# Reading TensorE's weights with a step in a gated attention and feed-forward kernel

## The chip, the cores and the metric

The kernel runs on one core of one Trainium2 chip. A core has TensorE (matrix products, into PSUM), VectorE, ScalarE and GpSimd (elementwise work), SyncE (which issues the transfers here), an on-chip memory SBUF of 128 partitions, and PSUM. In the profile they are PE, PEld (TensorE's loads of weights, which overlap its products), DVE, ACT, POOL and SP. A product takes two operands from SBUF: the weights, which are loaded into the array first (128 columns at most), and the moving operand, which then streams past them. The metric is the time of one execution on the device in microseconds; lower is better.

## The reference

Two blocks read the same x of 2048 tokens by 448, and a gate per token mixes them. Everything is float32.

```python
g = _sigmoid((x * gate_w).sum(-1, keepdims=True))
a = _A_ref(x, A_wqkv, A_wo)             # 16 heads of 28: softmax(q k^T * 28**-0.5) v, then @ wo
b = _B_ref(x, B_w_gate, B_w_up, B_w_down)   # (gelu(x @ w_gate) * (x @ w_up)) @ w_down, 1792 features
return g * a + (1 - g) * b
```

## The kernel before

**Precision.** Products that need float32 are made from two parts of each operand in a faster 32-bit type (float32r): a rounded part and the remainder. A product is then the sum of three: rounded by rounded, remainder by rounded, rounded by remainder. As the inner size 448 is three blocks of 128 and a half block of 64, the list `PAIRS` names eleven matmuls for one output tile: three pairs of blocks each for three combinations, and two in which the half block's two parts share 128 rows. So `X` has seven blocks of 2048 tokens (three rounded, one mixed, three remainders), and a weight tile has eight blocks of 128 columns. A tile that holds weights for a product and is followed by `LINE` (8) floats of padding is shifted against its neighbours by 32 bytes.

**Every matmul goes through the helper `mm` at L48**, which keeps them in the order of the program. So all products show L48 in the profile and are told apart by their tiles.

**Stage 1, queries, keys and values** (to about 117 us). `load_wqk` (L91 to L95) loads one of seven tiles of the q and k weights and splits it into `WQK`: ScalarE writes the rounded part (L94), VectorE the remainder (L95). `load_x` splits x into `X` (L107 to L114). `qk_tile` makes q and k with `WQK` as weights and `X` moving (group pqk, 7 tiles by 4 token blocks of 512, 11 matmuls each); the results go to memory. `v_tile` (L129 to L134) makes the values of 128 tokens with `X` as weights and `WV` moving (group pv, 16 tiles of 11 matmuls); column 448 of its result is the gate's argument.

**Stage 2, attention** (about 117 to 776 us). For each of 16 heads and 16 tiles of 128 keys, `scores` multiplies keys `K` (weights) with queries `Q` (moving), two matmuls for each half of the queries (group sc), and ScalarE takes the exponential (L265). `values` multiplies `V` (weights of 32 columns, four column groups side by side) with the exponentials; these operands are plain float32, and each such product is two instructions in the profile (group po). They are issued in batches for four key tiles at once. Between the scores, a generator `up` issues the up-projection of the feed-forward block, matmul by matmul, and three feature blocks of the gate projection: `half` tiles (one block of 128 features, split by `load_half`, L230 to L237, both halves by VectorE at L235 and L236) are the weights and `X` is moving (group pu, 68 tiles of 11 matmuls). The order of all this is written out in the loops; each `half` tile is loaded one feature block before it is used.

**Stage 3, gate, down and output** (about 776 us to the end). `hidden` makes the gate projection of the other 11 feature blocks (group pg, `half` tiles as weights, the rounded part written by ScalarE through `by_act` at L240), takes the gelu, multiplies by the up-projection and splits the product into `hl` (rounded and remainder, 512 tokens each). `down` multiplies `hl` (weights, 128 tokens at a time) with the down weights `w` (moving, 448 columns; group pd, 672 matmuls) and adds to `acc`, and after the last feature blocks writes out 128 tokens per transfer (L418). `load_o` and `project` do the attention's output projection with the split attention output `O` as weights and `WO` moving (group pd from ohl, 176 matmuls).

The matmuls' distance is what one counts in a chain that runs through TensorE: the start of one to the start of the next. The weights of a product are loaded while the product before it streams.

Of the kernel before, what the change touches and what calls it, by code (L numbers as in the profile page):

```python
# [7 lines left out]
F32 = mybir.dt.float32  # L8
# [3 lines left out]
OP = mybir.AluOpType  # L12
# [5 lines left out]
P = 128  # L18
TB = 512
# [8 lines left out]
RATE = 2  # L28
NB = 3
ORDER = (2, 3, 1, 4, 0, 5, 6)  # L30
NR = 4 * DH + 2
LINE = 8
VW = 450
# [4 lines left out]


PAIRS = [(b, w) for b in range(3) for w in (b, 4 + b)] + [(4 + b, b) for b in range(3)] + [(3, 3), (3, 7)]  # L40


@with_exitstack
def gated_mix(ctx: ExitStack, tc: tile.TileContext, xT, wqk, wvg, wg, wu, wd, wo, sel, ident, out):
    nc = tc.nc

    def mm(o, lhsT, rhs, start, stop):
        tc.keep_in_program_order(nc.tensor.matmul(o, lhsT, rhs, start=start, stop=stop))  # L48
# [10 lines left out]
    X = keep.tile([P, 7, S + LINE], F32R, name="X")  # L59
# [5 lines left out]
    kq = attn.enter_context(tc.tile_pool(name="kq", bufs=1))  # L65
    heads = [tuple(kq.tile([NR, S + (i + 1) * LINE], F32R, name=f"{x}{i}")[:, 0:S] for x in "QK")
             for i in range(2)]
# [5 lines left out]
    with ExitStack() as ph:  # L73
# [4 lines left out]
        psb = ph.enter_context(tc.tile_pool(name="psb", bufs=1, space=PSUM))  # L78

        WQKS = wp.tile([P, NQK, 8 * P + 2 * LINE], F32R, name="WQK")  # L80
        WQK = WQKS[:, :, 0:8 * P].rearrange("p t (w n) -> p t w n", w=8)
        WV = wp.tile([P, 8, VW], F32R, name="WV")
        selt = wp.tile([P, NQK, H], F32, name="selt")
        mx = wp.tile([P, NQK, NTB], F32, name="mx")
# [6 lines left out]
        def load_wqk(t):  # L91
            r = raw(wqk[t])
            r = r.rearrange("p (b n) -> p b n", b=4)
            nc.scalar.activation(WQK[:, t, 0:4], r, AF.Copy)  # L94
            nc.vector.tensor_tensor(WQK[:, t, 4:8], r, WQK[:, t, 0:4].bitcast(F32), OP.subtract)  # L95

# [19 lines left out]
        def qk_tile(t, tb):  # L116
            s = slice(tb * TB, (tb + 1) * TB)
            p = ps.tile([P, TB], F32, name="pqk")
            for i, (x, w) in enumerate(PAIRS):
                mm(p, WQK[:, t, w, :], X[:, x, s], i == 0, i == len(PAIRS) - 1)  # L120
            hl = st.tile([P, 2, TB], F32R, name="hl", bufs=3)
# [7 lines left out]
        def v_tile(i):  # L129
            p = psv.tile([P, VW], F32, name="pv")  # L130
            for j, (x, w) in enumerate(PAIRS):
                mm(p, X[:, x, i * P:(i + 1) * P], WV[:, w, :], j == 0, j == len(PAIRS) - 1)
            nc.scalar.activation(V[:, i, :, 0:DH], p[:, 0:D].rearrange("p (h d) -> p h d", h=H), AF.Copy)
            nc.vector.tensor_copy(gate[:, 0, i:i + 1], p[:, D:D + 1])  # L134

# [17 lines left out]
        for i in range(4):  # L153
            v_tile(i)
# [6 lines left out]
        for i in range(4, NT):  # L161
            v_tile(i)
# [6 lines left out]
        for a in range(2):  # L169
            nc.vector.tensor_copy(sh[:, a, :], hcol[:, a:a + 1].bitcast(F32).to_broadcast([H, P]))  # L170
            nc.sync.dma_start(out=shd[:, a].rearrange("h (i n) -> h i n", n=P),
                              in_=sh[:, a:a + 1].to_broadcast([H, NT, P]))
# [24 lines left out]
    with tc.If(bounded < 1):  # L197
        with ExitStack() as ph:
# [5 lines left out]
            for h in range(H):  # L204
                Q = gp.tile([4 * DH, S], F32R, name="gQ")
                K = gp.tile([4 * DH, S], F32R, name="gK")
# [3 lines left out]
                for i in range(NT):  # L210
                    p = gps.tile([P, S], F32, name="gsc")
                    for c in range(S // 512):
# [11 lines left out]
                                  in_=ms.bitcast(F32))  # L224
# [3 lines left out]
    halves = {}  # L228

    def load_half(src, f, key, hi):  # L230
        raw = fw.tile([P, 4, P], F32, name="hraw")
        w = fw.tile([P, 8 * P + LINE], F32R, name="half", bufs=3)
        w = w[:, 0:8 * P].rearrange("p (w n) -> p w n", w=8)
        nc.sync.dma_start(out=raw, in_=src[f])
        hi(w[:, 0:4], raw)  # L235
        nc.vector.tensor_tensor(w[:, 4:8], raw, w[:, 0:4].bitcast(F32), OP.subtract)  # L236
        halves[key, f] = w  # L237

    def by_act(o, i):
# [3 lines left out]
    with ExitStack() as ph:  # L243
# [14 lines left out]
        def scores(h, kt, half):  # L258
            Q, K = heads[h % 2]
            sc = psc.tile([P, 1024], F32, name="sc")  # L260
            for c in range(2):
                mm(sc[:, c * 512:(c + 1) * 512], K[:, kt * P:(kt + 1) * P],
                   Q[:, half * 1024 + c * 512:half * 1024 + (c + 1) * 512], True, True)
            pt = pp.tile([P, 1024], F32, name="pt")
            nc.scalar.activation(pt, sc, AF.Exp, scale=SCALE)  # L265
            PT[h, kt, half] = pt
# [29 lines left out]
        def up():  # L296

            todo = [(wu, f, "u") for f in range(NF)] + [(wg, f, "g") for f in range(NB)]
            load_half(*todo[0], nc.vector.tensor_copy)
            for n, (_, f, key) in enumerate(todo):  # L300
                for tb in range(NTB):
                    if tb == 1 and n + 1 < len(todo):
                        load_half(*todo[n + 1], nc.vector.tensor_copy)
                    s = slice(tb * TB, (tb + 1) * TB)
                    p = psu.tile([P, TB], F32, name="pu")
                    for i, (x, w) in enumerate(PAIRS):
                        mm(p, halves[key, f][:, w], X[:, x, s], i == 0, i == len(PAIRS) - 1)
                        if i < len(PAIRS) - 1:
                            yield False
                    u = op.tile([P, TB], F32, name="u")  # L310
                    nc.vector.tensor_copy(u, p)  # L311
                    nc.sync.dma_start(out=ud[n, :, s], in_=u)
                    yield True

        filler = up()

        hold = 0
# [9 lines left out]
        def spaced(h, kt, half):  # L327
            nonlocal hold
            scores(h, kt, half)
            hold = max(hold - 1, 0)  # L330
# [4 lines left out]
        for h in range(H):  # L335
            for kt in range(NKT):
                if kt == 2 and h + 1 < H:
                    load_head(h + 1)
                for half in range(2):
# [6 lines left out]
                    elif count != LATE - 1 or h + kt == 0:  # L346
                        first, last = h == 0 and kt <= ENDS[0] + 1, h == H - 1 and kt > ENDS[-2]
# [13 lines left out]
    with ExitStack() as ph:  # L361
# [9 lines left out]
        def load_f(f):  # L371
            if f >= NB:
                load_half(wg, f, "g", by_act)
            draw = gp.tile([P, D], F32, name="draw")
            w = gp.tile([P, 2 * D + LINE], F32R, name="w", bufs=3)
            w = w[:, 0:2 * D].rearrange("p (a n) -> p a n", a=2)
            nc.sync.dma_start(out=draw, in_=wd[f * P:(f + 1) * P])
            nc.scalar.activation(w[:, 0], draw, AF.Copy)
            nc.vector.tensor_tensor(w[:, 1], draw, w[:, 0].bitcast(F32), OP.subtract)
            WD[f] = w  # L380

        def hidden(f, tb, hl):
            s = slice(tb * TB, (tb + 1) * TB)
            u = tp.tile([P, TB], F32, name="u")
            nc.sync.dma_start(out=u, in_=ud[f, :, s])
            g = tp.tile([P, TB], F32, name="g")
            if f < NB:
                pg = tp.tile([P, TB], F32, name="gs")
                nc.sync.dma_start(out=pg, in_=ud[NF + f, :, s])
            else:  # L390
                pg = psg.tile([P, TB], F32, name="pg")
                for i, (x, w) in enumerate(PAIRS):
                    mm(pg, halves["g", f][:, w], X[:, x, s], i == 0, i == len(PAIRS) - 1)
            nc.scalar.activation(g, pg, AF.Gelu_apprx_tanh)  # L394
            nc.vector.tensor_tensor(g, g, u, OP.mult)  # L395
            nc.scalar.activation(hl[:, 0], g, AF.Copy)  # L396
            nc.vector.tensor_tensor(hl[:, 1], g, hl[:, 0].bitcast(F32), OP.subtract)  # L397

        def down(c, tb, hls):
            for i in range(4):  # L400
                t = tb * 4 + i
                s = slice(i * P, (i + 1) * P)
                p = psd.tile([P, D], F32, name="pd")
                n = 3 * len(hls)
                k = 0
                for f, hl in hls:
                    for a, b in ((0, 0), (1, 0), (0, 1)):
                        mm(p, hl[:, a, s], WD[f][:, b], k == 0, k == n - 1)
                        k += 1
                g1 = gate[:, 2, t:t + 1]  # L410
                if c == 0:
                    nc.vector.tensor_scalar(acc[:, t], p, g1, None, OP.mult)
                elif c < NF // FC - 1:
                    nc.vector.scalar_tensor_tensor(acc[:, t], p, g1, acc[:, t], OP.mult, OP.add)  # L414
                else:
                    y = tp.tile([P, D], F32, name="y")
                    nc.vector.scalar_tensor_tensor(y, p, g1, acc[:, t], OP.mult, OP.add)  # L417
                    nc.sync.dma_start(out=out[0, t * P:(t + 1) * P], in_=y)  # L418


        WO = wpo.tile([P, 8, D], F32R, name="WO")
# [23 lines left out]
        def project(tb):  # L445
            O = OHL[tb]
            for i in range(4):
                t = tb * 4 + i
                p = psd.tile([P, D], F32, name="pd")
                for k, (x, w) in enumerate(PAIRS):  # L450
                    mm(p, O[:, x, i * P:(i + 1) * P], WO[:, w], k == 0, k == len(PAIRS) - 1)
                nc.vector.scalar_tensor_tensor(acc[:, t], p, gate[:, 1, t:t + 1], acc[:, t], OP.mult, OP.add)

        order = [f for c in ORDER for f in range(c * FC, (c + 1) * FC)]
        load_f(order[0])
# [56 lines left out]
```

## Time and profile before

| | us |
|---|---|
| median of 3 runs | 1065.9 (1065.82 to 1066.63) |
| the profiled execution | 1066.95 |
| its span, first to last instruction | 1065.2 |
| TensorE busy in it | 1053.1 |
| ScalarE busy | 616.6 |
| VectorE busy | 320.8 |
| GpSimd busy | 41.1 |
| mean granted TensorE clock | 0.997 |

The profile is one execution, recorded by the hardware. A group of instructions is given as line, engine, operation, output<-inputs, shape and count, then busy microseconds, the mean nanoseconds of one, and the idle time of the engine before them with what ended it. Matmuls are pipelined and the ends of their records are modelled, so the mean duration of a matmul is longer than its share of the time. The chain that ended last is followed back from the last instruction, and a view of it in order of time merges neighbours of one group: start, microseconds, and how many. A view of stages gives, for each stretch of the span, its length, then the busy time of PE, PEld, DVE, ACT and POOL with counts, the granted clock, and the transfers' share.

### The profile page before, as it was taken

To read this page: it belongs to the slowest core of one execution; us is meant where nothing else is said; L and a number is where in the kernel's file an instruction comes from. 1 tells how busy PE (TensorE), PEld (TensorE's weight loads), DVE (VectorE), ACT (ScalarE), POOL (GpSimd) and SP (SyncE) were. 2 spreads that over 40 slices of the span, in tenths; PEclk is the share of its full clock that TensorE was granted. 3 is DMA by queue.
4 is the path that set the end of the run, shared out by engine and by line. 5 is a ranking of instruction groups with operands and counts; after the bars stand their busy time and mean duration, and the time that the engine had idled before them with its cause. 6 is when DMAs were issued, how large, how long until landed. Compare 5 with 4: busy or idle time off the path is not lost.

```text
span 1065.2 us, 14545 instructions
## 1 busy us (share of the span) xinstructions
PE 1053.1 (99%) x5664; PEld 733.4 (69%) x5664; DVE 320.8 (30%) x519; ACT 616.6 (58%) x732; POOL 41.1 (4%) x32
## 2 busy tenths in 40 slices
PE   7999999999999999999999999999999999999998
PEld 6889756556556556556566565565588888889887
DVE  6651111111111110110110110110157656577555
ACT  6422478778777777777787787787633332233321
POOL 5300000000000000000000000000001011100000
PEclk9999999999999999999999999999999999999999
DMA  8975222332332332332332232331164323342223
GB/s 278 302 262 121 59 73 73 120 103 73 100 106 73 96 110 73 94 112 73 94 112 74 94 111 74 94 102 42 59 192 138 106 88 94 92 148 67 62 85 118
DMA packets 58907, 115.85 MB, mean 109 GB/s; under 512 B 12784, under 2 KB 18160, under 8 KB 55216
## 3 DMA queue, kind: packets, MB, share of 16 engines
q1 hardware_dynamic: 58832, 114.85, 34.8%
q8 instruction: 47, 0.77, 0.3%
q14 instruction: 28, 0.23, 0.1%
HBM read 74.44 MB, written 40.37 MB: 108 GB/s over the span
## 4 chain that ended last, share of the span: by engine, by line
PE 88%; DVE 0%; issue 0%; DVEq 0%
PE sc L48 24%; PE po L48 21%; PE pu L48 16%; PE pd L48 16%; PE pg L48 11%; DVE u L311 0%; DVE y L417 0%; DVE gate L181 0%; DVE gate L180 0%; DVE gate L182 0%; DVEq L311 0%
## 5 line engine op out<-in xcount | busy, mean ns | idle before, releaser
L265 ACT ACTIVATE pt<-sc 128x1024 f32<-128x1024 f32 x512 | 482.3, 1026 | 165.3 <-PE sc L48 164.7
L48 PE MATMUL sc<-Q,K 114*128 114x512 f32 x1024 | 317.9, 402 | 1.3 <-issue 1.3
L48 PEld LDWEIGHTS sc<-Q,K 114*128 114x128 f32 x1024 | 188.8, 189 | 94.6 <-issue 54.5
L48 PE MATMUL pu<-X,half 128*128 128x512 f32 x748 | 238.3, 397 | 0.4 <-DVE u L311 0.3
L48 PE MATMUL po<-pt,V 128*32 128x512 f32 x2048 | 233.0, 595 | 0.0
L311 DVE COPY u<-pu 128x512 f32<-128x512 f32 x68 | 47.1, 692 | 493.2 <-PE pu L48 486.3
L48 PEld LDWEIGHTS pu<-X,half 128*128 128x128 f32 x748 | 141.4, 190 | 35.4 <-issue 1.4
L48 PEld LDWEIGHTS po<-pt,V 128*32 128x32 f32 x2048 | 60.0, 109 | 138.2 <-issue 132.4
L48 PE MATMUL pd<-w,hl 128*128 128x448 f32 x672 | 140.4, 365 | 0.0
L48 PEld LDWEIGHTS pd<-w,hl 128*128 128x128 f32 x672 | 126.1, 188 | 11.7
L48 PE MATMUL pg<-X,half 128*128 128x512 f32 x484 | 115.9, 394 | 0.0
L48 PEld LDWEIGHTS pg<-X,half 128*128 128x128 f32 x484 | 90.9, 188 | 20.1
L48 PE MATMUL pqk<-X,WQK 128*128 128x512 f32 x308 | 74.4, 404 | 6.0 <-ACT X L107 6.0
L48 PEld LDWEIGHTS pqk<-X,WQK 128*128 128x128 f32 x308 | 59.2, 193 | 20.7 <-ACT X L107 6.9
L394 ACT ACTIVATE g<-pg 128x512 f32<-128x512 f32 x44 | 26.2, 595 | 74.8 <-PE pg L48 74.7
L395 DVE TENSOR_TENSOR g<-g,u 128x512 f32<-128x512 f32 x56 | 46.4, 836 | 54.0 <-ACT g L394 53.5
L396 ACT ACTIVATE hl<-g 128x512 fp32r<-128x512 f32 x56 | 35.2, 630 | 42.9 <-DVE g L395 37.1
L414 DVE SCALAR_TENSOR_TENSOR acc<-pd,gate,acc 128x448 f32<-128x448 f32 x80 | 52.9, 679 | 6.3 <-PE pd L48 6.3
L442 POOL TENSOR_TENSOR ohl<-oraw,ohl 128x1536 fp32r<-128x1536 f32 x4 | 14.0, 3512 | 755.3 <-ACT ohl L438 755.3
L397 DVE TENSOR_TENSOR hl<-g,hl 128x512 fp32r<-128x512 f32 x56 | 38.3, 688 | 10.6 <-ACT hl L396 8.7
L48 PE MATMUL pv<-WV,X 128*128 128x450 f32 x176 | 36.8, 369 | 0.0
L48 PE MATMUL pd<-WO,ohl 128*128 128x448 f32 x176 | 36.6, 366 | 0.0
(60 smaller groups left out, 325.2 us busy)
## 6 DMA issues: line engine op xcount, KB each, us to landing
ud<-u SPq DMA_DIRECT2D x68, 256.0 KB
qkd<-hl SPq DMA_DIRECT2D x28, 512.0 KB
Q<-qkd SPq DMA_DIRECT2D x64, 224.0 KB
K<-qkd SPq DMA_DIRECT2D x64, 224.0 KB
u<-ud SPq DMA_DIRECT2D x56, 256.0 KB
raw<-in_xT SPq DMA_DIRECT2D x16, 256.0 KB
rb<-rdend SPq DMA_DIRECT2D x64, 64.0 KB
hraw<-in_wu SPq DMA_DIRECT2D x14, 256.0 KB
```

Source lines behind the costliest of these rows:

```text
L48: tc.keep_in_program_order(nc.tensor.matmul(o, lhsT, rhs, start=start, stop=stop))
L265: nc.scalar.activation(pt, sc, AF.Exp, scale=SCALE)
L311: nc.vector.tensor_copy(u, p)
L394: nc.scalar.activation(g, pg, AF.Gelu_apprx_tanh)
L395: nc.vector.tensor_tensor(g, g, u, OP.mult)
L396: nc.scalar.activation(hl[:, 0], g, AF.Copy)
L397: nc.vector.tensor_tensor(hl[:, 1], g, hl[:, 0].bitcast(F32), OP.subtract)
L414: nc.vector.scalar_tensor_tensor(acc[:, t], p, g1, acc[:, t], OP.mult, OP.add)
L442: nc.gpsimd.tensor_tensor(O[:, 4:7], o[:, 0:3], O[:, 0:3].bitcast(F32), OP.subtract)
```

## The change

Every float32r operand that serves as weights of a product is read with a step between its columns. Moving operands stay as they were.

- `WQK`: the eight blocks of a tile are interleaved column by column, so that the 128 columns of a block lie 8 floats (32 bytes) apart. ScalarE and VectorE write them in this way.
- `half` tiles: within each of four blocks the rounded part and the remainder alternate, so columns lie 2 floats (8 bytes) apart; the two writers write with that step.
- `X` in `v_tile`, `K` in `scores`, `hl` in `down` and `O` in `project`: the layout stays, and the 128 tokens of a tile are no longer neighbours but every fourth of a block of 512 (`tokens`), 4 floats (16 bytes) apart. The rows of `V`, the gate and `acc` follow this order, and the transfers of the output write every fourth row.

`V` in `values` is weights too and stays as it was. The padding stays.

```diff
+def tokens(i):
+    first = i // 4 * TB + i % 4
+    return slice(first, first + 4 * (P - 1) + 1, 4)
...
-        WQK = WQKS[:, :, 0:8 * P].rearrange("p t (w n) -> p t w n", w=8)
+        WQK = WQKS[:, :, 0:8 * P].rearrange("p t (n w) -> p t w n", w=8)
...
-                mm(p, X[:, x, i * P:(i + 1) * P], WV[:, w, :], j == 0, j == len(PAIRS) - 1)
+                mm(p, X[:, x, tokens(i)], WV[:, w, :], j == 0, j == len(PAIRS) - 1)
...
-        w = w[:, 0:8 * P].rearrange("p (w n) -> p w n", w=8)
+        w = w[:, 0:8 * P].rearrange("p (b n a) -> p a b n", b=4, a=2)
         nc.sync.dma_start(out=raw, in_=src[f])
-        hi(w[:, 0:4], raw)
-        nc.vector.tensor_tensor(w[:, 4:8], raw, w[:, 0:4].bitcast(F32), OP.subtract)
+        hi(w[:, 0], raw)
+        nc.vector.tensor_tensor(w[:, 1], raw, w[:, 0].bitcast(F32), OP.subtract)
...
-                mm(sc[:, c * 512:(c + 1) * 512], K[:, kt * P:(kt + 1) * P],
+                mm(sc[:, c * 512:(c + 1) * 512], K[:, tokens(kt)],
                    Q[:, half * 1024 + c * 512:half * 1024 + (c + 1) * 512], True, True)
...
-                        mm(p, halves[key, f][:, w], X[:, x, s], i == 0, i == len(PAIRS) - 1)
+                        mm(p, halves[key, f][:, w // 4, w % 4], X[:, x, s], i == 0, i == len(PAIRS) - 1)
...
-                    mm(pg, halves["g", f][:, w], X[:, x, s], i == 0, i == len(PAIRS) - 1)
+                    mm(pg, halves["g", f][:, w // 4, w % 4], X[:, x, s], i == 0, i == len(PAIRS) - 1)
...
-                s = slice(i * P, (i + 1) * P)
+                s = tokens(i)
...
-                    nc.sync.dma_start(out=out[0, t * P:(t + 1) * P], in_=y)
+                    nc.sync.dma_start(out=out[0, tokens(t)], in_=y)
...
-                    mm(p, O[:, x, i * P:(i + 1) * P], WO[:, w], k == 0, k == len(PAIRS) - 1)
+                    mm(p, O[:, x, tokens(i)], WO[:, w], k == 0, k == len(PAIRS) - 1)
```

## The prediction

> **What bounds the kernel now.** I read the page from the top: busy times, the slices with the granted clock, the chain that ended last, then the groups.
>
> ```profile
> span 1065.2 us, 14545 instructions
> PE 1053.1 (99%) x5664; PEld 733.4 (69%) x5664; DVE 320.8 (30%) x519; ACT 616.6 (58%) x732; POOL 41.1 (4%) x32
> ...
> PEclk9999999999999999999999999999999999999999
> ...
> PE 88%; DVE 0%; issue 0%; DVEq 0%
> PE sc L48 24%; PE po L48 21%; PE pu L48 16%; PE pd L48 16%; PE pg L48 11%; DVE u L311 0%; DVE y L417 0%; DVE gate L181 0%; DVE gate L180 0%; DVE gate L182 0%; DVEq L311 0%
> ```
>
> TensorE is busy 99% of the span at the full granted clock, and the chain runs from matmul to matmul with nearly nothing else in it. So the kernel gets shorter only if the distance from one matmul to the next shrinks, and longer as soon as it grows. The number of matmuls stays as it is. The next view is the groups: the matmuls, and the weight loads (PEld) that run beside them.
>
> ```profile
> L48 PE MATMUL sc<-Q,K 114*128 114x512 f32 x1024 | 317.9, 402 | 1.3 <-issue 1.3
> L48 PE MATMUL pu<-X,half 128*128 128x512 f32 x748 | 238.3, 397 | 0.4 <-DVE u L311 0.3
> L48 PE MATMUL po<-pt,V 128*32 128x512 f32 x2048 | 233.0, 595 | 0.0
> L48 PEld LDWEIGHTS po<-pt,V 128*32 128x32 f32 x2048 | 60.0, 109 | 138.2 <-issue 132.4
> L48 PE MATMUL pd<-w,hl 128*128 128x448 f32 x672 | 140.4, 365 | 0.0
> L48 PEld LDWEIGHTS pd<-w,hl 128*128 128x128 f32 x672 | 126.1, 188 | 11.7
> L48 PE MATMUL pg<-X,half 128*128 128x512 f32 x484 | 115.9, 394 | 0.0
> L48 PEld LDWEIGHTS pg<-X,half 128*128 128x128 f32 x484 | 90.9, 188 | 20.1
> L48 PE MATMUL pqk<-X,WQK 128*128 128x512 f32 x308 | 74.4, 404 | 6.0 <-ACT X L107 6.0
> L48 PE MATMUL pv<-WV,X 128*128 128x450 f32 x176 | 36.8, 369 | 0.0
> L48 PE MATMUL pd<-WO,ohl 128*128 128x448 f32 x176 | 36.6, 366 | 0.0
> ```
>
> The edit reaches every group here but po, whose weights V stay as they are: pu and pg (748 + 484 = 1232, the half tiles, step 8 bytes); sc, pv and both pd (1024 + 176 + 672 + 176 = 2048, step 16); pqk (308, step 32). That is 3588 matmuls: 2564 with 512 moving columns (sc, pu, pg, pqk), and 1024 with 448 or 450 (pd, pv). A mean duration (394) is no distance, as matmuls overlap. The distances stand in the chain by time, in a stretch where gate matmuls and down matmuls alternate:
>
> ```profile
> 841.05 5.09 PE pg L48 x22
> 846.14 4.88 PE pd L48 x24
> ```
>
> 5.09/22 = 231.4 ns for 512 columns, 4.88/24 = 203.3 ns for 448. The difference, 28.0 ns over 64 columns, is 0.438 ns a column. 512 columns at that are 224.3, so 7.1 ns of each matmul do not go with its columns. This line through two points is one measure of what each matmul pays beside its stream. A second comes from po, in the timeline of TensorE, where sixteen of its instructions are four rounds of four side by side:
>
> ```profile
> 235.88 1.90 PE L48 MATMUL po<-pt,V 128*32 128x512 f32 x16
> ```
>
> The last round lasts about the mean of 0.595, so a round takes (1.90 - 0.595)/3 = 0.435 us for 512 columns. These operands are plain float32, and one such instruction lasts 595 - 397 = 198 ns longer than pu's with as many columns. I read that as two steps per column against one, which makes a bare stream of 512 columns 435/2 = 217.5 ns: an estimate, and 231.4 - 217.5 = 13.9 ns less than pg's distance. So 7 to 14 ns in each of the 3588 matmuls are not explained by columns. In po a weight load brings 32 columns; in the other groups a load of 128 columns goes beside every stream.
>
> [...]
>
> **The change, part by part.** *Weight loads.* No instruction is added or removed; 3588 loads read their 128 columns 2, 4 or 8 elements apart while the moving operand is read as before. No row shows an operand read or written with a step, so this is the unknown cost, and I bound it from both sides. On the good side, the unexplained time of each matmul may be the load and the stream in each other's way in the memory; a load that hops through it no longer walks behind the stream in the same place. What it can give back is between 7.1 and 13.9 ns a matmul: 25.5 to 49.9 us. I take the middle, 10.5 ns: 3588 x 10.5 = 37.7 us. The middle, because the two measures have equal weight: the line through two points counts what depends on columns as lost for good, the other calls everything above po's rate removable. On the bad side a column may take longer to read, or both collide more often; those are the rivals, and their ends stand there.
>
> *Writes with a step.* load_wqk writes 7 + 7 times with step 32, load_half 28 times with step 8.
>
> ```profile
> L94 ACT ACTIVATE WQK<-raw 128x512 fp32r<-128x512 f32 x7 | 4.3, 629 | 2.4 <-DMA raw<-in_wqk 2.3
> L95 DVE TENSOR_TENSOR WQK<-raw,WQK 128x512 fp32r<-128x512 f32 x7 | 4.6, 687 | 4.7 <-ACT WQK L94 4.6
> L235 DVE CAST half<-hraw 128x512 fp32r<-128x512 f32 x17 | 7.1, 418 | 0.0
> L236 DVE TENSOR_TENSOR half<-hraw,half 128x512 fp32r<-128x512 f32 x28 | 19.3, 691 | 7.4 <-ACT half L240 6.9
> L240 ACT ACTIVATE half<-hraw 128x512 fp32r<-128x512 f32 x11 | 6.9, 629 | 7.5 <-PE pu L48 7.4
> ```
> ```profile
> 0.00:20.00 20.00, 14.00 (x49) 10.73 (x50) 12.10 (x17) 13.60 (x22) 10.62 (x12) 1.00 0.76 248
> ...
> 117.00:776.00 659.00, 657.27 (x3825) 390.73 (x3824) 87.41 (x150) 485.39 (x519) 0.00 (x0) 1.00 0.29 89
> 776.00:1056.00 280.00, 280.00 (x1310) 245.72 (x1309) 176.56 (x263) 89.15 (x142) 16.88 (x8) 1.00 0.36 107
> ```
> ```profile
> 3.50 0.63 ACT L94 ACTIVATE WQK<-raw 128x512 fp32r<-128x512 f32 x1 [1.47 <-DMA raw<-in_wqk]
> 4.78 0.63 ACT L107 ACTIVATE X<-raw 128x512 fp32r<-128x512 f32 x1 [0.66 <-DMA raw<-in_xT]
> 5.47 1.22 PE L48 MATMUL pqk<-X,WQK 128*128 128x512 f32 x2 [5.47 <-ACT X L107]
> ```
>
> The second fence is the stages: span, then busy PE, PEld, DVE, ACT, POOL. Each write may stay as it is or, as the far end, take twice its time. The half tiles then cost DVE up to 7.1 + 19.3 = 26 us more and ACT 7, spread over 935 us in which DVE is busy for 264 and ACT for 574; each tile is loaded a whole feature block ahead. That work is hidden by the matmuls of the block before, so I cost it at nothing; without that cover its price would be those 33 us. The WQK tiles are needed at the start, where PE is idle for 6 of 20 us: ACT idled 0.66 us between the first WQK tile and X, so that tile's doubling just fits, and the first matmul waits for X. The other six could push ACT back by 6 x 0.63 = 3.8 us, while PE works through the first tiles. Between 0 and 3.8 us I take 0.6, one such copy, as PE has 11 matmuls per tile to cover the rest.
>
> *Steps taken from a whole block* (X, K, hl, O): tokens(i) picks every fourth token of the same 512, so each matmul waits for the tiles it waited for before; no DMA, wait or queue entry is added, and none is moved past another. *Output*: the same 16 transfers, their rows now 4 tokens apart in memory.
>
> ```profile
> out<-y SPq DMA_DIRECT2D x16, 224.0 KB
> ```
>
> Rows of 448 floats stay whole; only the last one is bare, and with rows as long as before I take 0 (between 0 and 1 us). *What comes next when matmuls move closer*: ScalarE's exponentials, 512 of 1026 ns.
>
> ```profile
> L265 ACT ACTIVATE pt<-sc 128x1024 f32<-128x1024 f32 x512 | 482.3, 1026 | 165.3 <-PE sc L48 164.7
> ```
> ```profile
> 235.50 3.57 PE po L48 x32
> ...
> 245.59 3.57 PE po L48 x32
> ```
>
> A round of the attention lasts 245.59 - 235.50 = 10.09 us and holds 8 exponentials, 8.2 us. Besides po's 3.57 us it holds 28 matmuls; 14 ns off each make 9.7 us, still above 8.2. ScalarE does not become the bound.
>
> *Sum*: the profiled execution took 1066.95 us (span 1065.2 and 1.75 around it), 1.05 above the median of the runs, 1065.9. 1066.95 - 37.7 + 0.6 = 1029.9, and against the median 1028.8: I say 1029.
>
> **The rivals.** *The read becomes the bound (slower).* Loads of 128 columns take 188 ns, po's of 32 take 109: (188 - 109)/96 = 0.82 ns a column, 105 for 128. In the groups a load of pd leaves 11.7 us/672 = 17 ns idle, one of pg 20.1/484 = 42. If a load must end before its matmul starts, the distance grows once a column costs 17/128 = 0.14 ns more. Were a column read to take twice as long, a load would be 293 and the distance 293 + 17 = 310: 1332 matmuls of 512 (sc, pqk) lose 78.6, 1024 of pd and pv 106.7, together 214 us, so 1280. For it: pd's small idle time. Against it: loads overlap one another where they may.
>
> ```profile
> L48 PEld LDWEIGHTS pr<-selt,sq 128*1 128x1 f32 x14 | 0.4, 81 | 0.0
> ```
>
> 14 loads of 81 ns lie in 0.4 us, so the fixed 81 is latency, and only the 105 must fit: doubled, 210 against 203.3, 7 ns for 1024 matmuls, 1073. I price both. [...]
>
> *More collisions (slower).* The 7.1 ns may be the price of the memory that a load touches, which grows to 2, 4 and 8 times: 7.1 x (1232 x 1 + 2048 x 3 + 308 x 7) = 67.7 us, 1134; at 13.9 ns 1198. For it: the loads are the only thing each of these matmuls has beside its stream. Against it: nothing shows that the price goes with the stretch.
>
> *Nothing happens.* If loads and streams never meet, the distance stays and only the start changes: 1066.5. [...] The unexplained 7 to 14 ns speak against, without naming the load.
>
> **How the numbers follow.** Faster, with 1029 and a range of its own from 1005 (17 ns a matmul: 14, and 3 for rounding and for the starts of a round's four that lie apart) to 1055: 0.60. Unchanged: 0.08. The read as bound, strictly (1280): 0.11; overlapped (1073): 0.08. More collisions (1134 and above): 0.13. A difference under 0.2%, 2.1 us, can't be told from none. So faster 0.60, same 0.08, slower 0.32. From 1005 to 1135 the range leaves out the strict bound (0.11), half of the collisions (0.06) and 0.03 below.
>
> **What would show it.** Right: pg's 22 matmuls in the chain near 4.86 us and pd's 24 near 4.63, po's 32 still 3.57, loads still 188. Wrong: loads well over 188 in sc and pd but not in pu (the read binds); loads of 188 with pg's 22 above 5.09 (collisions); ACT or DVE waiting for WQK in the first 20 us (writes); or an idle PE in the attention with ScalarE full. The weakest step is the first: that the unexplained time belongs to the load at all.

## The result and the profile after

The changed kernel takes 1115.45 us (median of 4 runs, 1114.6 to 1116.13) against 1066.27 for the kernel before (median of 4): the ratio is 1.0458, 95% interval 1.044 to 1.0476, or 48.8 us more (4.58% of 1066.27; the costs of the other kernels below are worked out from their ratios in the same way). The forecast was 1029, so it had the wrong sign. TensorE is busy for 99% of the span as it was, and the clock is the same:

```profile
span 1114.1 us, 14545 instructions
PE 1101.6 (99%) x5664; PEld 867.5 (78%) x5664; DVE 327.6 (29%) x519; ACT 622.9 (56%) x732; POOL 42.2 (4%) x32
...
PEclk9999999999999999999999999999999999999999
...
PE sc L54 23%; PE po L54 21%; PE pd L54 18%; PE pu L54 16%; PE pg L54 10%; DVE u L317 0%; DVE y L423 0%; DVE gate L187 0%; DVE gate L186 0%; DVE gate L188 0%; DVEq L317 0%
...
L54 PE MATMUL sc<-Q,K 114*128 114x512 f32 x1024 | 329.1, 413 | 1.3 <-issue 1.3
L54 PEld LDWEIGHTS sc<-Q,K 114*128 114x128 f32 x1024 | 275.0, 311 | 69.5 <-issue 54.5
L54 PE MATMUL pu<-X,half 128*128 128x512 f32 x748 | 239.9, 400 | 0.3
L54 PE MATMUL pd<-w,hl 128*128 128x448 f32 x672 | 161.3, 397 | 0.0
L54 PEld LDWEIGHTS pd<-w,hl 128*128 128x128 f32 x672 | 160.0, 330 | 0.8
L54 PEld LDWEIGHTS pg<-X,half 128*128 128x128 f32 x484 | 94.9, 196 | 16.8
L54 PE MATMUL pqk<-X,WQK 128*128 128x512 f32 x308 | 78.5, 418 | 6.6 <-ACT X L113 5.7
L54 PEld LDWEIGHTS pqk<-X,WQK 128*128 128x128 f32 x308 | 76.5, 329 | 8.2 <-ACT X L113 7.1
L54 PE MATMUL pv<-WV,X 128*128 128x450 f32 x176 | 42.0, 400 | 0.0
```

(Lines have moved by six: L54 is the helper `mm`.) Weight loads are what changed. With steps of 16 and 32 bytes they last 311 to 332 ns instead of 188 to 193; with 8 bytes 196 to 197. The chain in order of time, in the stretch that the prediction used, gives the distances:

```profile
835.60 5.13 PE pg L54 x22
840.73 5.62 PE pd L54 x24
846.35 5.12 PE pg L54 x22
```

The gate matmuls, with half tiles as weights, are where they were: 5.12/22 = 233 ns against 231. The down matmuls went from 203.3 to 5.62/24 = 234.2. One more place grows, the first pair of score matmuls behind a batch of po. In the timeline of the kernel before, no load had run for 0.84 us ahead of such a pair's first one, so there is nothing that it overlaps. Here is the pair before, behind the batch that begins at 235.50, and one after:

```profile
239.07 0.67 PE sc L48 x2
239.73 0.47 PE pu L48 x2
```
```profile
237.27 3.57 PE po L54 x32
240.84 0.80 PE sc L54 x2
241.64 0.47 PE pu L54 x2
```

The sum by groups, for pd the difference of the distances, for the others that of the mean durations: pd 848 x 30.9 ns = 26.2 us, pv 176 x 31 = 5.5, sc 1024 x 11 = 11.3 (8.3 of it the 64 first pairs, 0.13 each), pqk 308 x 14 = 4.3, pu and pg 2.7. Together 50.0, against 48.9 by the spans.

### The profile page after: what moved, and what is told of

It is laid out like the page before. It is cut to its first block, busy times and chain, and to the rows that moved or that the text cites. A ratio compares the mean times of both kernels' runs of the same rounds, so it can differ in the third digit from the quotient of the medians.

```text
span 1114.1 us, 14545 instructions
## 1 busy us (share of the span) xinstructions
PE 1101.6 (99%) x5664; PEld 867.5 (78%) x5664; DVE 327.6 (29%) x519; ACT 622.9 (56%) x732; POOL 42.2 (4%) x32
## 4 chain that ended last, share of the span: by engine, by line
PE 88%; DVE 0%; issue 0%; DVEq 0%
PE sc L54 23%; PE po L54 21%; PE pd L54 18%; PE pu L54 16%; PE pg L54 10%; DVE u L317 0%; DVE y L423 0%; DVE gate L187 0%; DVE gate L186 0%; DVE gate L188 0%; DVEq L317 0%
## 5 line engine op out<-in xcount | busy, mean ns | idle before, releaser
L54 PE MATMUL sc<-Q,K 114*128 114x512 f32 x1024 | 329.1, 413 | 1.3 <-issue 1.3
L54 PEld LDWEIGHTS sc<-Q,K 114*128 114x128 f32 x1024 | 275.0, 311 | 69.5 <-issue 54.5
L54 PE MATMUL pu<-X,half 128*128 128x512 f32 x748 | 239.9, 400 | 0.3
L54 PE MATMUL po<-pt,V 128*32 128x512 f32 x2048 | 233.0, 595 | 0.0
L54 PEld LDWEIGHTS po<-pt,V 128*32 128x32 f32 x2048 | 60.0, 109 | 130.7 <-issue 127.0
L54 PE MATMUL pd<-w,hl 128*128 128x448 f32 x672 | 161.3, 397 | 0.0
L54 PEld LDWEIGHTS pd<-w,hl 128*128 128x128 f32 x672 | 160.0, 330 | 0.8
L54 PEld LDWEIGHTS pu<-X,half 128*128 128x128 f32 x748 | 147.0, 197 | 15.8 <-issue 1.4
L54 PE MATMUL pg<-X,half 128*128 128x512 f32 x484 | 116.4, 395 | 0.0
L54 PEld LDWEIGHTS pg<-X,half 128*128 128x128 f32 x484 | 94.9, 196 | 16.8
L54 PE MATMUL pqk<-X,WQK 128*128 128x512 f32 x308 | 78.5, 418 | 6.6 <-ACT X L113 5.7
L54 PEld LDWEIGHTS pqk<-X,WQK 128*128 128x128 f32 x308 | 76.5, 329 | 8.2 <-ACT X L113 7.1
L400 ACT ACTIVATE g<-pg 128x512 f32<-128x512 f32 x44 | 26.2, 596 | 86.7 <-PE pg L54 86.6
L54 PE MATMUL pd<-WO,ohl 128*128 128x448 f32 x176 | 42.1, 398 | 0.0
L54 PE MATMUL pv<-WV,X 128*128 128x450 f32 x176 | 42.0, 400 | 0.0
L54 PEld LDWEIGHTS pd<-WO,ohl 128*128 128x128 f32 x176 | 41.9, 332 | 0.0
```

## The experiments

Two theories stood at the start. *Slow read*: a column that lies 16 bytes or more from the last one takes about twice as long to read; reads overlap the stream before, and a matmul waits only where its stream is shorter than the read. *Collisions*: a load with a step disturbs the stream beside it. A third question was what the 7 to 14 ns were that the prediction had set out to win.

**A table of patterns (scan).** Extra matmuls into a PSUM bank that nothing reads, 24 for each pattern, for 64 and then 512 moving columns:

```diff
+        for N in (64, 512):
+            for k in range(24):
+                keep_(nc.tensor.matmul(px[0:P, 0:N], step(k % 7, 1), X[:, (k + 3) % 7, 0:N], start=True, stop=True))
...
+            for k in range(24):
+                keep_(nc.tensor.matmul(px[0:P, 0:N], step(k % 7, 16), X[:, (k + 3) % 7, 0:N], start=True, stop=True))
```

> The kernel before with 768 extra matmuls behind the values of stage 1, into a PSUM bank that nothing reads: for 64 and then for 512 moving columns, sixteen patterns of 24 each. Weights from X with steps of 1, 1 (one float further on), 2, 2 (one float further on), 3, 4, 5, 6, 8 and 16 floats, then 32 and 64 columns side by side, then step 1 with a moving operand that is one column repeated, step 1 with a moving operand read with step 2, and bfloat16 weights with steps of 2 and of 16 bytes. Slow read (the read of a column takes about twice as long once its neighbour lies 16 bytes away or more, and reads overlap the stream before): at 64 moving columns the distance is the read alone, about 109 ns for steps 1 and 2, 230 to 245 for 4 and above, 3 in between; at 512 columns 232 for steps 1 and 2 and 235 to 245 from 4 on. Collisions (a stepped load delays the stream and is not slower itself): at 64 columns all steps about 109, at 512 columns a distance that grows from step to step. On the unexplained 7 to 14 ns: if they belong to the load, 32 columns in place of 128 bring 512 moving columns from 232 to about 218; if they are the two operands meeting in the memory, the repeated column does so too; if they belong to neither, both stay at 232.

In the part with 64 columns the granted clock falls to half behind the first pattern, as the view of stages shows in its third column from the end. L174 is the first pattern, step 1 (in floats), still at the full clock; L184 is step 4, at half of it.

```profile
120.00:123.00 3.00, 3.00 (x27) 2.94 (x25) 0.76 (x4) 0.76 (x2) 0.00 (x0) 1.00 0.00 0
138.00:143.00 5.00, 5.00 (x25) 5.00 (x25) 0.00 (x0) 0.00 (x0) 0.00 (x0) 0.50 0.00 0
```
```profile
120.58 2.76 PE L174 MATMUL px<-X 128*128 128x64 f32 x24
143.44 5.79 PE L184 MATMUL px<-X 128*128 128x64 f32 x24
```

24 matmuls are 23 distances and one duration, so a distance is (busy - mean)/23, good to about 2 ns. The load sets it here, as weights of 32 columns in place of 128 bring it to some 54 ns (L194). It is 108 ns for step 1 at the full clock (mean duration 273 ns). At half the clock it is 213 ns for step 1 (L198, whose weights are side by side) and for steps 2 and 3, but 234 for 4 (mean 420), 223 for 5 and 6, 239 for 8 and 218 for 16. At the full clock step 4 takes 235 as well (L213 of the second table below). So a load of columns side by side took twice as long at half the clock (213 ns against 108), and a load of columns 16 bytes apart did not get longer (234 against 235). Collisions had expected the same distance for all steps.

The part with 512 runs at the full clock (1.00 from 190 to 240 us). Groups by line, loads first: busy, then the mean of one. L176 is step 1 from one float further on (the first pattern, L174, ran into the change of the clock), L178 step 2, L182 step 3, L184 step 4, L186 step 5, L190 step 8, L192 step 16 (in floats).

```profile
L190 PEld LDWEIGHTS px<-X 128*128 128x128 f32 x24 | 6.0, 330 | 0.0
L186 PEld LDWEIGHTS px<-X 128*128 128x128 f32 x24 | 5.8, 305 | 0.0
L192 PEld LDWEIGHTS px<-X 128*128 128x128 f32 x24 | 5.7, 301 | 0.0
L184 PEld LDWEIGHTS px<-X 128*128 128x128 f32 x24 | 5.7, 310 | 0.0
L182 PEld LDWEIGHTS px<-X 128*128 128x128 f32 x24 | 5.6, 253 | 0.0
L178 PEld LDWEIGHTS px<-X 128*128 128x128 f32 x24 | 4.6, 194 | 0.9
L176 PEld LDWEIGHTS px<-X 128*128 128x128 f32 x24 | 4.5, 188 | 1.1
```

Less the fixed 81 ns that the prediction read from pr, 128 columns take 107 ns at step 1, 113 at 2, 172 at 3, 229 at 4, 220 to 249 above. In pieces of 16 bytes these are 32, 64, 96 and 128 pieces: 113/64, 172/96 and 229/128 are all 1.8 ns a piece. So these float32r loads took the larger of 0.83 ns a column (107/128) and about 1.8 ns a piece; beyond one column per piece the step changed it by no more than a tenth (218 to 239 ns at 64 columns), and what makes this difference is open. In L213, where the load holds the matmuls up, its record is longer (331 ns, 250 less 81, at a distance of 235), so there the distance is the better measure. The bfloat16 patterns of the table do not fit this: their 128 columns loaded in 98 ns when side by side and in 144 when 16 bytes apart, although the latter touch 128 pieces too (L202 and L204, at 512 columns). With 512 columns the distance is 231 to 239 ns at every step but that of 32 bytes, 247; it does not grow from step to step as collisions asked.

The same table's matmuls answer the third question (L198: the moving operand is one column repeated; L194: weights of 32 columns; L200: a moving operand of step 2):

```profile
L200 PE MATMUL px<-X 128*128 128x512 f32 x24 | 11.1, 634 | 0.0
L176 PE MATMUL px<-X 128*128 128x512 f32 x24 | 5.8, 396 | 0.0
L194 PE MATMUL px<-X 128*32 128x512 f32 x24 | 5.7, 394 | 0.0
L198 PE MATMUL px<-X 128*128 128x512 f32 x24 | 5.3, 379 | 0.0
```

By (busy - mean)/23 the distances are L176 235 ns, L194 231, L198 214, L200 455. A quarter of the weights changes next to nothing; a moving operand that reads one place gives back the whole excess (214), and so does one of bfloat16, half the bytes (L204, 5.3 us and 379 ns: 214); one that touches twice the memory took about twice the time (455). What the prediction wanted to win belongs to the moving operand's own reading, not to the load.

**Each part alone (halves8, k16, xo16, wqk32).** The kernel before with one part of the change:

```diff
 halves8
-        w = w[:, 0:8 * P].rearrange("p (w n) -> p w n", w=8)
+        w = w[:, 0:8 * P].rearrange("p (b n a) -> p a b n", b=4, a=2)
 k16
-                mm(sc[:, c * 512:(c + 1) * 512], K[:, kt * P:(kt + 1) * P],
+                mm(sc[:, c * 512:(c + 1) * 512], K[:, tokens(kt)],
 xo16
-                mm(p, X[:, x, i * P:(i + 1) * P], WV[:, w, :], j == 0, j == len(PAIRS) - 1)
+                mm(p, X[:, x, tokens(i)], WV[:, w, :], j == 0, j == len(PAIRS) - 1)
-                s = slice(i * P, (i + 1) * P)
+                s = tokens(i)
-                    mm(p, O[:, x, i * P:(i + 1) * P], WO[:, w], k == 0, k == len(PAIRS) - 1)
+                    mm(p, O[:, x, tokens(i)], WO[:, w], k == 0, k == len(PAIRS) - 1)
 wqk32
-        WQK = WQKS[:, :, 0:8 * P].rearrange("p t (w n) -> p t w n", w=8)
+        WQK = WQKS[:, :, 0:8 * P].rearrange("p t (n w) -> p t w n", w=8)
```

> The half tiles alone with their step of 8 bytes. Slow read: two columns still lie within 16 bytes, loads of 196 ns instead of 188, pg's 22 matmuls stay at 5.10 us, the time within 2 us of the kernel before. Collisions: the cost goes with the memory touched, 9 of 68 parts of the 49 us that the change cost: about 6 us more.

> The keys alone with a step of 16 bytes; the values keep their order, so keys meet the values of other tokens and the sums differ. Slow read: the score matmuls hide most of the longer read behind 512 moving columns; 4 ns for 1024 of them and, behind each of 64 batches of po, whose column tiles a load does not overlap, one load laid bare, 0.13 us each: 12 us more. Collisions: the same price for every matmul with a step of 16 bytes, 1024 of 2356 for some 40 us: 18 us more.

> X in the values, gelu products and attention output with their step of 16 bytes, keys and the weights of q, k and half tiles as before; keys meet the values of other tokens, so the sums differ. Slow read: the 1024 matmuls of 448 or 450 columns go from 203 and 206 ns to 234, the time of the read: 31 us more. Collisions: 1024 of 2356 for some 40 us: 18 us more.

> The weights of q and k alone with a step of 32 bytes, written so by ScalarE and VectorE too. Pieces: 128 x 1.87 = 239 ns a load, the distance in pqk goes from 232 to 245, 308 x 13 ns = 4 us more, and up to 1 us at the start where the writes take longer. If the writes were the cost, pqk would stay near 232 and the idle time before it would grow by the 4 us.

| kernel | us | ratio to before (95%) | slow read expected | measured |
|---|---|---|---|---|
| halves8 | 1068.28 | 1.0009 (0.9999 to 1.0018) | within 2 us | +1.0 |
| k16 | 1079.63 | 1.0117 (1.01 to 1.0134) | +12 | +12.5 |
| xo16 | 1099.51 | 1.0304 (1.0287 to 1.0321) | +31 | +32.4 |
| wqk32 | 1070.57 | 1.004 (1.0025 to 1.0055) | +4 to 5 | +4.3 |

The parts add up to 50.2 us, the change cost 48.8. The sizes that were expected for the slow read came from the profile after the change, so this table shows where the loss lies and that little else adds to it; the length of the read itself is shown by the tables of patterns. Collisions asked for 6, 18 and 18 in the first three and missed each. In the chain of xo16 the down matmuls grow as they did in the change, while the gate matmuls stay; 31 ns for each of its 1024 matmuls make 31.7 of its 32.4 us:

```profile
835.09 5.62 PE pd L53 x24
840.71 5.11 PE pg L53 x22
```

In wqk32 the matmuls themselves became longer (mean 404 before, 418 here), and TensorE's idle time ahead of them hardly did (6.0 and 6.8; it is 7.1 to 7.8 in halves8, k16 and xo16, which write WQK as before), so the writes with a step are not the cost:

```profile
L48 PE MATMUL pqk<-X,WQK 128*128 128x512 f32 x308 | 78.9, 418 | 6.8 <-ACT X L107 5.7 <-DVE mx L124 1.2
```

**All steps 8 bytes (all8).**

```diff
-    first = i // 4 * TB + i % 4
-    return slice(first, first + 4 * (P - 1) + 1, 4)
+    first = i // 2 * 2 * P + i % 2
+    return slice(first, first + 2 * (P - 1) + 1, 2)
...
-        WQK = WQKS[:, :, 0:8 * P].rearrange("p t (n w) -> p t w n", w=8)
+        WQK = WQKS[:, :, 0:8 * P].rearrange("p t (b n a) -> p t a b n", b=4, a=2)
```

> The whole change with steps of 8 bytes alone: tokens(i) takes every second token of 256, and the weights of q and k alternate rounded part and remainder. Pieces: 64 pieces a load, 64 x 1.83 = 117 ns in place of 107, so loads of 196 to 197 everywhere and no matmul held by them: within 3 us of the kernel before, 46 us faster than the change. If any step cost something in itself, or the order of tokens or the output's rows did, half of the loss or more would stay: 1090.

1069.66 us, ratio 1.0032 (1.0019 to 1.0045): 3.4 us above the kernel before, a little over the 3 that were expected, and 46 below the change (against 1115.45, which was not measured beside it). Two columns per piece make loads of 195 to 196 ns, pd's 24 matmuls stay at 4.88 us in the chain, and the reordered tokens and output rows are all in this kernel too, so they cost next to nothing. It is no gain either.

```profile
L54 PEld LDWEIGHTS sc<-Q,K 114*128 114x128 f32 x1024 | 195.5, 196 | 88.8 <-issue 54.7 <-ACT pt L271 0.6
L54 PEld LDWEIGHTS pd<-w,hl 128*128 128x128 f32 x672 | 130.9, 195 | 7.6
```

**The moving operand's pieces (scan2).** If a piece costs 1.8 ns, the moving operand must show it: 512 float32r columns are 128 pieces.

```diff
+        def wrap(b, h, c=4):
+            return X[:, b, 0:512].rearrange("p (a l c) -> p l a c", l=h, c=c)
...
+        for k in range(24):
+            keep_(nc.tensor.matmul(px, X[:, k % 7, 0:P], wrap((k + 3) % 7, 4), start=True, stop=True))
...
+        for k in range(24):
+            keep_(nc.tensor.matmul(px[:, 0:256], X[:, k % 7, 0:509:4], X[:, (k + 3) % 7, 0:256], start=True, stop=True))
```

> The kernel before with 456 extra matmuls behind the values of stage 1, into a PSUM bank that nothing reads, weights side by side; what varies is the moving operand, from X: 512 columns side by side; the same one float further on; 16-byte pieces (4 columns) with 2, 3 and 4 pieces from one to the next; one block of 512 columns read in another order, in pieces of 16 bytes with 2, 4, 8, 16, 32 and 64 pieces from one to the next; in pieces of 32 bytes with 2, 4 and 8 of them from one to the next; in pieces of 64 bytes with 4 from one to the next; 16-byte pieces from four blocks in turn; then 448 and 256 columns side by side, and 256 with weights of step 16 bytes. Pieces (both operands are read in pieces of 16 bytes at about 1.8 ns each, and a matmul takes the longest of its own 216 ns, its 128 moving pieces and its weights' pieces): 512 columns 231, one float further on, with 129 pieces, 233; the period depends on the distance of the pieces as it did for weights (1.83 ns at one piece, 1.87 at two, 1.70 at four), so 239 at two, 218 at four; 448 columns 203, 256 columns 116, and 256 with stepped weights 234. A fixed cost per matmul in place of it: 231 in all orders, 256 columns 123 to 125.

L177 is 512 columns side by side, L189 the same block with 4 pieces from one to the next, L193 with 16, L185 pieces with 4 from one to the next over a longer stretch, L211 256 columns, L213 256 columns with weights of step 16 bytes:

```profile
L193 PE MATMUL px<-X 128*128 128x512 f32 x24 | 6.8, 445 | 0.0
L185 PE MATMUL px<-X 128*128 128x512 f32 x24 | 5.9, 402 | 0.0
L213 PE MATMUL px<-X 128*128 128x256 f32 x24 | 5.8, 397 | 0.0
L177 PE MATMUL px<-X 128*128 128x512 f32 x24 | 5.8, 396 | 0.0
L189 PE MATMUL px<-X 128*128 128x512 f32 x24 | 5.5, 384 | 0.0
L211 PE MATMUL px<-X 128*128 128x256 f32 x24 | 3.0, 280 | 0.0
```

By (busy - mean)/23: 235 ns for 512 side by side, 118 for 256, half of it. So there is no fixed cost per matmul that would show; 118/64 and 235/128 are 1.84 ns a piece. L213 is the change in small: 235 ns for 256 columns, whose stream alone takes 118, because the read of the stepped weights sets the distance. The order of pieces matters, but not as expected from the weights: 222 with 4 pieces inside a block (expected 218), 231 with 2 (expected 239), 276 with 16, and 239 with 4 over the longer stretch, where 218 was expected. That expectation, whose numbers were the 234, 239 and 218 ns of the stepped loads, is a miss: a period by the distance of two pieces alone doesn't hold. No run shows the 216 ns that the expectation gave a matmul of 512 columns by itself; the repeated column of the first table took 214 (L198).

**Another order of the moving operand (scan3, order4).**

```diff
     def mm(o, lhsT, rhs, start, stop):
+        n = rhs.shape[-1]
+        if rhs.dtype == F32R and n % 16 == 0:
+            o = o.rearrange("p (a l c) -> p l a c", l=4, c=4)
+            rhs = rhs.rearrange("p (a l c) -> p l a c", l=4, c=4)
         tc.keep_in_program_order(nc.tensor.matmul(o, lhsT, rhs, start=start, stop=stop))
```

> As the second table of patterns, 432 extra matmuls, now on the order of the moving operand's 16-byte pieces and of the output: 512 columns side by side; read with 4 pieces from one to the next; the same with the output written in that order too, so that no column changes its place; the output alone written so; pieces of 32 bytes with 4 from one to the next; 4 pieces with weights of step 8 bytes; then 448 columns side by side, with 4 pieces, with 4 for the output too, with 7, 14, 2 and 28; then 480 columns with 3, 5, 6 and 4 pieces and side by side. Pieces, of which the order sets the period: 234, 223, 223, 234; 448 columns 203 side by side and 195 with 4 pieces. If the output's order costs its own time, the third and fourth are above the second and first.

In the third table L171 is 512 columns side by side, L173 with 4 pieces from one to the next, L175 the same with the output in that order; L183 is 448 columns side by side and L187 the same with 4 pieces and the output in that order:

```profile
L171 PE MATMUL px<-X 128*128 128x512 f32 x24 | 5.8, 396 | 0.0
L173 PE MATMUL px<-X 128*128 128x512 f32 x24 | 5.5, 385 | 0.0
L175 PE MATMUL px<-X 128*128 128x512 f32 x24 | 5.5, 384 | 0.0
L183 PE MATMUL px<-X 128*128 128x448 f32 x24 | 5.0, 365 | 0.0
L187 PE MATMUL px<-X 128*128 128x448 f32 x24 | 4.9, 360 | 0.0
```

The output's order costs nothing that shows (222 with and without it), 448 columns gain about 4 ns (201 to 197) where 8 were expected.

> The kernel before, its weights side by side as they were; the matmuls of 512 and 448 float32r columns read the moving operand's 16-byte pieces with 4 pieces from one to the next and write the output's columns in the same order, so nothing else changes. Pieces: 10 ns less for 2564 matmuls of 512 columns and 8 ns for 848 of 448, 32 us faster: 1034. If the output's order is what a matmul then waits for, or the gain of 4 pieces holds only for the addresses of that table, no change or slower.

1049.42 us, ratio 0.9834 (0.982 to 0.9848): 17.7 us faster than the kernel before, and the best of all. Half of what was expected: in its chain pd's 24 matmuls take 4.77 us, 199 ns each, and pg's 11 take 2.50, 227, where the third table gave 197 and 222.

```profile
841.78 4.77 PE pd L52 x24
846.55 2.50 PE pg L52 x11
```

Why it is half, and why some orders are faster and others slower, is open; whether it depends on where both operands lie in the memory was not taken apart.

## Why the prediction was wrong

*What bounds the kernel*: right. TensorE is busy 99% in both, and the loss is in the distances alone, in groups that the sum of the result accounts for.

*The step that failed is the good side of "Weight loads"*, the 10.5 ns a matmul, 37.7 us in all, that a stepped load was to give back. The runs show in its place that a load with a step of 16 or 32 bytes gets longer, and sets the distance wherever the stream is shorter: 31 ns more for each of 1024 matmuls of 448 or 450 columns, 32 of the 49 us. The sign that the prediction named for this came: loads well over 188 ns in sc and pd (311 and 330), not in pu (197).

What misled it is that it took the time not explained by columns for the load's. Weights of 32 columns leave 231 of 235 ns, and a repeated moving column brings 214: the excess is the moving operand's pieces, which the edit does not touch. The line through two points misled in particular. 231.4 and 203.3 ns over 128 and 112 pieces are 1.81 and 1.815 ns each, a line through the origin. Its constant is eight times the shorter distance less seven times the longer, so small errors grow: the stretches of the chain before run from 231 to 233 ns (pg x22, 5.08 to 5.13 us) and from 202 to 205 (pd x24, 4.85 to 4.91), and with these the constant lies anywhere from -15 to 23. They can't tell 7 ns from none, and 256 columns (118 ns) decide it. The comparison with po measured a real excess of about 14 ns, but named nobody for it, as the prediction said of its weakest step.

*The read becomes the bound*: this rival happened, in its overlapped form (0.08, 1073). Its mechanism was right: loads of 330 ns stand in distances of 234, so only a part of each must fit. Its size was off. The read was taken to double, 210 ns, and took 234 to 235 at 16 bytes and up to 247 at 32 (L190); so 1024 matmuls of 448 or 450 columns lost 31 ns instead of 7, 32 us. Two terms were missing: 308 matmuls of pqk, which at 32 bytes lost 14 ns, and the 64 loads behind a batch of po, laid bare for 0.13 us each. The strict form (1280) is refuted by the same rows, as it asked for distances of 310. The loads of float32r weights lasted 194 to 197 ns at 8 bytes, 253 at 12 and 301 to 332 from 16 on. The moving operand behaved otherwise: at 8 bytes, two columns to a 16-byte piece, 512 columns took 455 ns, and side by side, with four, still 235 against the 214 of one repeated column. The chance for this rival, 0.19 in both forms, was too small: a row spoke for it (pd's 17 ns of idle), and no row named the load for the good side.

*More collisions*: refuted by halves8, k16 and xo16, whose prices go with the stream's length and not with the memory touched: for the same step of 16 bytes 12 ns a matmul at 512 columns, most of it in the bare loads, and 32 at 448 or 450. *Nothing happens*: its condition, that loads and streams never meet, fits within 4 ns: 512 columns took 235 ns beside loads of 128 columns (L176 of the first table), 231 beside loads of 32 (L194) and 235 at step 4 (L184). What it left out is that the load itself can become too long (235 ns for a stream of 118, L213).

*Writes with a step*: within the bounds. In the groups of the changed kernel WQK's two writers nearly double (629 to 1188, 687 to 1156 ns), the half tiles' three grow by 1 to 8% (418 to 422, 691 to 704, 629 to 682). That the matmuls hide the half tiles' writes was right (the 935 us over which the prediction spread them are 659 + 280 = 939, which changes nothing):

```profile
L101 DVE TENSOR_TENSOR WQK<-raw,WQK 128x512 fp32r<-128x512 f32 x7 | 7.8, 1156 | 5.0 <-ACT WQK L100 4.9
L100 ACT ACTIVATE WQK<-raw 128x512 fp32r<-128x512 f32 x7 | 7.7, 1188 | 1.8 <-DMA raw<-in_wqk 1.7
L242 DVE TENSOR_TENSOR half<-hraw,half 128x512 fp32r<-128x512 f32 x28 | 19.7, 704 | 7.5 <-ACT half L246 6.9
L241 DVE CAST half<-hraw 128x512 fp32r<-128x512 f32 x17 | 7.2, 422 | 0.0
```

TensorE's idle time before pqk went from 6.0 to 6.6 us, the 0.6 that the sum had for the start; that match is luck, as the same idle time is 7.1 to 7.8 us in halves8, k16 and xo16, which write WQK as before. What these writes cost is lost in that scatter. *Tokens and output rows at no cost*: right within the 3.4 us of all8, which has them all. *ScalarE does not become the bound*: not put to the test by a slower kernel; in order4, 17.7 us faster, TensorE is still busy for 99% of the span.

## What to carry to other kernels

Ask of a stall that no row explains which operand it follows, before forecasting that a change to the other one removes it; a table of bare matmuls with one thing varied at a time costs one run. Here weights of float32r 8 bytes apart cost 3.4 us in all (all8), but from 16 bytes on a load of 128 columns took 218 to 247 ns; it held up the matmuls whose stream is shorter (203 ns at 448 columns, 118 at 256) and, by 0.13 us each, the 64 first pairs behind a batch of po, whose loads nothing covers. And where a float32r stream is the bound, the order in which the moving operand is read is worth trying: here it gave 1.7% (order4).

## What the runs showed of the hardware

- Both float32r operands of TensorE were read at about 1.8 ns for each 16-byte piece: weights 113, 172 and 229 ns for 64, 96 and 128 pieces (scan; side by side 0.83 ns a column set it, 107 ns), the moving operand 118, 203, 231 to 235 and 455 ns for 64, 112, 128 and 256 (scan2, the chain before, scan). A repeated column streamed 512 in 214 (scan). Weights of bfloat16 were not held so: loads of 144 ns at 16 bytes, 98 side by side (scan).
- A load of 128 float32r columns 16 bytes apart took 234 ns at a granted clock of 0.50 (scan) and 235 at 1.00 (scan2); side by side it took 213 and 108 (scan).
- The order of pieces changed the moving operand's period: 512 columns in 222 ns with 4 pieces from one to the next inside the block, 276 with 16 (scan2).
- While matmuls of 64 columns ran in a row, the granted clock fell from 1.00 (120 to 123 us of scan) to 0.54 (123 to 128) and 0.50 (138 to 149), though TensorE was busy by the profile for all of these stretches; with 512 columns it was 1.00 again (190 to 240).
